# A planned instruction order for a recurrent attention and a mixing layer, searched again with other costs

## The chip, the cores and the metric

The kernel runs on one core of one Trainium2 chip. The metric is the device time of one execution in microseconds (us). The core's engines work side by side, each on its own queue of instructions in a fixed order: TensorE (PE, matmuls; PEld is its loading of weights), VectorE (DVE), ScalarE (ACT), GpSimd (POOL) and SyncE (SP, which here only issues DMAs). An instruction waits on semaphores for what other engines or DMAs have to finish first, and everything behind it in its queue waits too.

## The reference, cut to what matters

Two layers follow each other. The first is a recurrence over 768 tokens for 4 batches and 8 heads of width 48, the second mixes tokens and channels:

```python
for t in range(S):                       # r, k, v: [4, 8, 768, 48]
    cur = einsum('bhd,bhe->bhde', u[None] * kt, vt)
    y[:, :, t] = einsum('bhd,bhde->bhe', rt, state + cur)
    state = w[None, :, :, None] * state + einsum('bhd,bhe->bhde', kt, vt)
x = y.transpose(0, 2, 1, 3).reshape(4, 768, 384)
theta = x @ w_theta
zr, zi = x * cos(theta), x * sin(theta)
y = einsum('ts,bsd->btd', w_tok_r, zr) + einsum('ts,bsd->btd', w_tok_i, zi)
u = x + y
out = u + maximum(u @ w_ch, 0.0)         # float32
```

## The kernel before, in words

**Tiling.** The 768 tokens of a batch are three pairs of chunks of 128. The twelve pairs of the four batches are numbered g0 to g11; three make a batch. For each pair the recurrence is done in blocks. k and r are loaded (`ld`) and multiplied by tables of powers of the decay into `Kw` and `Rw` (line 677, "products"); eight 128x128 blocks of each are turned on TensorE (line 566, "flip") and copied out of PSUM as `KT` and `RT` (lines 575 and 577). `scores` (line 716) are KT times RT, masked by VectorE into `mAT` (line 723). `PD` (line 730) is the elementwise product of RT and KT; `diag` (line 739) sums it into a small bank that ScalarE copies as `dg`, and `yd` (line 747) is dg times v, the term with u. `outer` (lines 762 and 776) makes the pair's contribution to the state, and `Sb1`, `T`, `N` and `Sb0` carry the state on. `past` (line 836) and `outputs` (line 847) make the result, and `x` (line 855) adds yd. v is cast to bf16 as `vb` (lines 616 and 618); for g0 to g3, whose loads take two tokens to a partition, it is cast as `v2` (line 630), sorted by TensorE (`put`, line 641) and copied out (`put out`, lines 649 and 651).

The second layer takes x of a pair, turns it (on TensorE, or for g6 to g10 by a DMA that SP issues, "turn", line 586), multiplies by w_theta (`theta`, line 870), takes cosine and sine on ScalarE (lines 875 and 878) and multiplies x by both on VectorE (`z`, line 881). When z of a pair is there, a third of the token mixing of its batch can run: `mix` (line 901) is four matmuls of 384 columns, three such parts for each of six row blocks of 128 tokens. `un` (line 908) adds x, a DMA turns it (TensorE for g11), `chan` (line 924) multiplies by w_ch and `fin` (line 928) makes the output, which SP stores.

**Weights.** w_theta, w_tok_r, w_tok_i and w_ch are cast to bf16 by DMAs that GpSimd issues (line 523), behind a `gate` (line 701), a copy of one element that waits for the eighth load. Each cast of w_tok brings two row blocks (01, 23 or 45), which TensorE turns and ScalarE or VectorE copies out.

**What sets the order.** The kernel is first written down as 710 tasks with engine, cost, reads, writes and PSUM banks (`P.add`). `RANK` gives each task a priority and `MOVED` names the tasks that go to their other engine (`Plan.move`: copies out of PSUM, casts of v, products, PD and yd each have one). `Plan.order` then plays the program through with the planner's costs: an engine that is free takes, of the tasks that are ready, the one with the lowest priority value. The result is the order in which the instructions are written. The costs matter only for this. `act_ns`, `dve_ns` and `pool_ns` give them by the number of elements, a task on TensorE costs 1.9 times as much before `SLOW_UNTIL`, and of tasks marked `port=True` VectorE and GpSimd never run two at once in the plan. When the instructions are written, the first such GpSimd instruction after a VectorE one is made to wait for it (`add_manual_dep`, in the last loop); VectorE gets no such wait for GpSimd. `fill` (line 969) puts matmuls on a constant tile (`stuff`) where `replay` finds TensorE idle early on; their number in a gap goes by `FREE_FROM`.

Of the kernel before, what the change touches and what calls it, by code (L numbers as in the profile page):

```python
# [22 lines left out]
PE, DVE, ACT, POOL, SP = "PE", "DVE", "ACT", "POOL", "SP"  # L23
# [3 lines left out]
FILL_FIRST = 6  # L27
FILL_UNTIL = 17500.0
FREE_FROM = 7400.0
SLOW_UNTIL = 10400.0  # L30
TURN_LATE = 1300.0


# [6 lines left out]
class Plan:  # L40
# [50 lines left out]
    def order(self):  # L91
# [23 lines left out]
        while times or dma_next < math.inf:  # L115
# [26 lines left out]
            for e in engines:  # L142
# [14 lines left out]
                if e == PE:  # L157
                    ns += SWITCH if t.mode != last_mode else 0.0
                    ns *= 1.9 if now < SLOW_UNTIL else 1.0
                    last_mode = t.mode  # L160
# [33 lines left out]
CAST_AFTER = 7  # L194

RANK = [
# [38 lines left out]
]  # L235

MOVED = [
    32, 50, 74, 89, 97, 128, 165, 185, 198, 200, 213, 218, 225, 230, 246, 248, 249, 280, 285,
    358, 370, 371, 403, 405, 436, 448, 513, 526, 531, 573, 591, 606, 703,
]  # L240


# [8 lines left out]
def bc(ap, axis, n):  # L251
    new_ap = [list(x) for x in ap.ap]
    new_ap.insert(axis, [0, n])
    return dataclasses.replace(ap, ap=new_ap)
# [3 lines left out]
def kernel(  # L258
# [13 lines left out]
    nc = tc.nc  # L272
    B, H, S, D = r.shape
    HD = H * D
# [10 lines left out]
    P = Plan(8)  # L285
# [70 lines left out]
    def dve_ns(n, rate=1.0):  # L356
        return n / (0.96 * rate) + 66

    def pool_ns(n):
        return 190 + 1.95 * n  # L360

    def setup():
        P.add(SP, 420, lambda: nc.sync.dma_start(out=w_f, in_=w.rearrange("(o h) d -> o (h d)", o=1)),
# [232 lines left out]
    def front(b, base):  # L596
# [3 lines left out]
        for pr in range(NP):  # L600
# [24 lines left out]
            def cast2(eng, v2=v2, iv=slots[pr][2]):  # L625
# [5 lines left out]
                else:  # L631
                    eng.tensor_copy(dst, src)
            P.add(ACT, act_ns(2 * HD, False), lambda f=cast2: f(nc.scalar),
                  rd=both(slots[pr][2]), wr=[("v2", i2)], prio=base + 10 * pr + 1, name="v2",
                  alt=(POOL, pool_ns(2 * HD) - 200, True, lambda f=cast2: f(nc.gpsimd)))
            for c in range(2):
                tv = ("V", g, c)
# [18 lines left out]
        for pr in range(NP):  # L656
# [205 lines left out]
            xT, trig = xTs[g % 2], trigs[g % 2]  # L862
            turn(xT.rearrange("p t d c -> p (t d) c"), x[:, 2 * pr:2 * pr + 2],
                 ("TX", g), pb + 7, xk, [("xT", g % 2)], g in X_BY_DMA)
            for t in range(2):
                th = ("th", g, t)

                def theta(th=th, t=t, xT=xT):
# [9 lines left out]
                P.add(ACT, act_ns(HD) + 35, lambda th=th, t=t, trig=trig: nc.scalar.activation(  # L878
                    trig[:, t, 1], bank(th)[:, :HD], Act.Sin), use=[th],
                    wr=[("trig", g % 2, t, 1)], prio=pb + 8, name="sin")  # L880
            P.add(DVE, dve_ns(4 * HD, 2.0) + 80, lambda trig=trig, pr=pr: nc.vector.tensor_mul(  # L881
                z[:, 2 * pr:2 * pr + 2], bc(x[:, 2 * pr:2 * pr + 2], 2, 2), trig),
                rd=xk + [("trig", g % 2, t, i) for t in range(2) for i in range(2)],
                wr=[("z", zj, pr)] + (["w_f", "lw_f"] if g == NP else []), prio=pb + 9, port=True, name="z")
# [54 lines left out]

    setup()  # L940
    front(0, 0)
    for b in range(B):
        if b + 1 < B:
            front(b + 1, 100 * (b + 1))
        mixing(b, 100 * b + 150)
# [51 lines left out]
    for t in order:  # L997
# [8 lines left out]
        n = len(made)  # L1006
# [39 lines left out]
```

## Time and profile before

| | |
|---|---|
| median of 3 runs (lowest, highest) | 139.09 us (139.02, 139.81) |
| the profiled execution | 139.07 us, span 137.4 us, mean granted TensorE clock 0.996 |
| busy PE, DVE, ACT, POOL | 125.3, 112.3, 73.1, 62.5 us |
| moved by DMA | 25.24 MB, 184 GB/s on average |
| chain that ended last | PE 49%, DMA 17%, DVE 14%, POOL 9% |

The span runs from the first to the last instruction; the time of an execution holds 1.67 us more. "Busy" is the time in which an instruction of the engine was under way, which may include time in which it could not go on. The matmuls' ends are modelled: a matmul of 384 columns is shown with 0.326 us, and the next one starts 0.163 us after it. A row of the timeline gives start, length, engine, line, operation, tiles written and read, and in brackets how long the engine stood idle before it and what ended that. A row of a group gives count, busy time and the mean length in ns, then idle time before it.

### The profile page before, as it was taken

To read this page: it belongs to the slowest core of one execution; us is meant where nothing else is said; L and a number is where in the kernel's file an instruction comes from. 1 tells how busy PE (TensorE), PEld (TensorE's weight loads), DVE (VectorE), ACT (ScalarE), POOL (GpSimd) and SP (SyncE) were. 2 spreads that over 40 slices of the span, in tenths; PEclk is the share of its full clock that TensorE was granted. 3 is DMA by queue.
4 is the path that set the end of the run, shared out by engine and by line. 5 is a ranking of instruction groups with operands and counts; after the bars stand their busy time and mean duration, and the time that the engine had idled before them with its cause. 6 is when DMAs were issued, how large, how long until landed. Compare 5 with 4: busy or idle time off the path is not lost.

```text
span 137.4 us, 4145 instructions
## 1 busy us (share of the span) xinstructions
PE 125.3 (91%) x1698; PEld 84.9 (62%) x1698; DVE 112.3 (82%) x210; ACT 73.1 (53%) x137; POOL 62.5 (46%) x56
## 2 busy tenths in 40 slices
PE   1989888989999999999899997999899999999970
PEld 1567665776677667767566665776566666566640
DVE  6299999997888799998999999999855799454390
ACT  7996699999565660869334226457550092500010
POOL 7037999956080958776579909690000000000000
PEclk9999999999999999999999999999999999999998
DMA  2999999999979999999999999999991432526235
GB/s 69 235 325 325 315 194 198 196 196 202 219 153 237 154 224 105 207 199 185 180 149 224 165 229 225 199 250 175 197 289 36 88 107 95 139 93 172 57 149 195
DMA packets 72637, 25.24 MB, mean 184 GB/s; under 512 B 67241, under 2 KB 72618, under 8 KB 72618
## 3 DMA queue, kind: packets, MB, share of 16 engines
q1 hardware_dynamic: 70186, 22.03, 81.2%
q0 software_dynamic: 2432, 2.95, 12.5%
q8 instruction: 13, 0.21, 0.6%
q14 instruction: 6, 0.05, 0.1%
HBM read 20.06 MB, written 4.72 MB: 180 GB/s over the span
## 4 chain that ended last, share of the span: by engine, by line
PE 49%; DMA 17%; DVE 14%; POOL 9%; SPq 5%; issue 3%; ACT 1%; POOLq 0%; DVEq 0%
PE bank L901 24%; DMA z<-in_moe_w_tok_r_dram 7%; PE bank L566 6%; PE bank L870 6%; DMA ld<-in_v_dram 6%; PE bank L924 5%; SPq L503 4%; DVE mAT L723 4%; DMA ld<-in_r_dram 4%; POOL Rw L677 3%; DVE fin_all L928 2%; POOL yd L747 2%; PE bank L716 2%; PE bank L847 2%; PE bank L762 2%
## 5 line engine op out<-in xcount | busy, mean ns | idle before, releaser
L901 PE MATMUL bank<-z,WrT 128*128 128x384 bf16 x144 | 46.9, 326 | 0.0
L901 PE MATMUL bank<-z,WiT 128*128 128x384 bf16 x144 | 46.8, 326 | 0.0
L723 DVE TENSOR_TENSOR mAT<-bank,mask 128x512 bf16<-128x512 f32 x48 | 30.7, 680 | 1.4 <-PE bank L716 1.3
L677 POOL TENSOR_TENSOR Kw<-ld,kpow 128x768 bf16<-128x768 f32 x9 | 16.3, 1816 | 12.7 <-DVE PD L730 6.4
L908 DVE TENSOR_TENSOR uu_all<-bank,x 128x384 bf16<-128x384 f32 x24 | 13.3, 552 | 8.8 <-PE bank L901 8.3
L677 POOL TENSOR_TENSOR Rw<-ld,rpow 128x768 bf16<-128x768 f32 x9 | 16.4, 1820 | 7.1 <-DMA ld<-in_r_dram 3.4
L901 PEld LDWEIGHTS <-WrT 128*128 128x128 bf16 x144 | 14.0, 98 | 8.0
L901 PEld LDWEIGHTS <-WiT 128*128 128x128 bf16 x144 | 14.1, 98 | 7.8
L747 POOL TENSOR_TENSOR yd<-dg,vb 128x768 bf16<-128x768 f32 x10 | 14.7, 1477 | 6.8 <-DVE z L881 4.0
L878 ACT ACTIVATE trig<-bank 128x384 f16<-128x384 f32 x24 | 11.6, 494 | 10.2 <-PE bank L870 10.2
L928 DVE SCALAR_TENSOR_TENSOR fin_all<-bank,uu_all 128x384 f32<-128x384 f32 x24 | 12.6, 551 | 3.4 <-PE bank L924 3.4
L875 ACT ACTIVATE trig<-bank,pi 128x384 f16<-128x384 f32 x24 | 13.7, 584 | 1.9 <-PE bank L870 1.9
L870 PE MATMUL bank<-Wth,xT 128*128 128x384 bf16 x72 | 14.4, 326 | 0.4 <-DMA Wth<-in_moe_w_theta_dram 0.4
L924 PE MATMUL bank<-Wch,uu_all 128*128 128x384 bf16 x72 | 14.6, 326 | 0.0
L881 DVE TENSOR_TENSOR z<-x,trig 128x1536 bf16<-128x1536 bf16 x12 | 12.8, 1063 | 0.4 <-ACT trig L875 0.4
L855 DVE TENSOR_TENSOR x<-bank,yd 128x384 bf16<-128x384 f32 x24 | 12.3, 547 | 0.7 <-POOL yd L747 0.5
L577 ACT ACTIVATE KT<-bank 128x1024 bf16<-128x1024 bf16 (+1 forms) x10 | 9.8, 980 | 4.9 <-PE bank L566 3.9
L577 ACT ACTIVATE RT<-bank 128x1024 bf16<-128x1024 bf16 (+1 forms) x9 | 8.8, 976 | 4.2 <-PE bank L566 4.2
L924 PEld LDWEIGHTS <-uu_all 128*128 128x128 bf16 x72 | 6.7, 98 | 3.9
L566 PE MATMUL bank<-ident,Rw 128*128 128x128 bf16 x96 | 7.6, 220 | 1.6 <-DVE fin_all L928 0.8
L716 PE MATMUL bank<-RT,KT 64*128 64x128 bf16 x192 | 8.8, 218 | 0.0
L870 PEld LDWEIGHTS <-xT 128*128 128x128 bf16 x72 | 6.3, 97 | 4.0 <-issue 0.4
(108 smaller groups left out, 190.7 us busy)
## 6 DMA issues: line engine op xcount, KB each, us to landing
ld<-in_r_dram SPq DMA_DIRECT2D x12, 384.0 KB, 5.9
out_dram<-fin_all SPq DMA_DIRECT2D x11, 384.0 KB, 2.7
ld<-in_k_dram SPq DMA_DIRECT2D x16, 192.0 KB, 5.7
ld<-in_v_dram SPq DMA_DIRECT2D x16, 192.0 KB, 5.2
ld<-in_k_dram SPq DMA_DIRECT2D x4, 384.0 KB, 4.8
ld<-in_v_dram SPq DMA_DIRECT2D x4, 384.0 KB, 5.0
fin_all<-in_moe_w_tok_r_dram POOLq DMA_DIRECT2D x1, 384.0 KB, 8.6
x<-in_moe_w_tok_i_dram POOLq DMA_DIRECT2D x1, 384.0 KB, 10.1
```

The source lines that it names most:

```text
L566: nc.tensor.matmul(bank16(tok)[:, i * C:(i + 1) * C], s, ident, is_transpose=True, start=(i == 0), stop=(i == n - 1))
L577: nc.scalar.activation(dst, src, Act.Copy)
L677: eng.tensor_mul(X[:, :, hs, :D], src[:, :, hs], pw[:, :, hs])
L723: P.add(DVE, dve_ns(HP * C), lambda hi=hi, tk=tk, mAT=mAT: nc.vector.tensor_mul(mAT[:, hi], bank(tk[hi]).rearrange("p (h t) -> p h t", h=H ...
L747: eng.tensor_mul(yd.rearrange("p a h d -> p (a h) d"), wide(dg, D), vb.rearrange("p a h d -> p (a h) d"))
L870: nc.tensor.matmul(bank(th)[:, :HD], xT[:, t, dk, :], Wth[:, dk, :], start=(dk == 0), stop=(dk == ND - 1))
L875: P.add(ACT, act_ns(HD, False) + 65 + (1300 if g == 0 and t == 0 else 0), lambda th=th, t=t, trig=trig: nc.scalar.activation(trig[:, t, 0] ...
L881: P.add(DVE, dve_ns(4 * HD, 2.0) + 80, lambda trig=trig, pr=pr: nc.vector.tensor_mul(z[:, 2 * pr:2 * pr + 2], bc(x[:, 2 * pr:2 * pr + 2], ...
L901: nc.tensor.matmul(bank(tm)[:, :HD], (WrT, WiT)[ri][:, so, to * C:(to + 1) * C], z[:, so, ri], start=(part == 0 and i == 0), stop=(part == ...
L908: P.add(DVE, dve_ns(HD), lambda tm=tm, t=t, to=to, un=un: nc.vector.tensor_add(un[:, t], bank(tm)[:, :HD], x[:, to]), use=[tm], rd=[("x", ...
L924: nc.tensor.matmul(bank(tf)[:, :HD], uT[:, t, dk, :], Wch[:, dk, :], start=(dk == 0), stop=(dk == ND - 1))
L928: nc.vector.scalar_tensor_tensor(fin[:, t], bank(tf)[:, :HD], 0.0, un[:, t], op0=Alu.max, op1=Alu.add),
```

## The change

The planner's costs are changed in three places: TensorE is slow until 7400 ns instead of 10400, GpSimd's products cost 2.06 ns per element instead of 1.95, and VectorE's z costs 80 ns less. With these costs RANK and MOVED were searched anew, and both lists are replaced. Nothing that the tasks compute is changed.

```diff
-SLOW_UNTIL = 10400.0
+SLOW_UNTIL = 7400.0
@@ RANK: all 710 values replaced
-    0, 463, 462, 465, 464, 466, 467, 468, 471, 474, 479, 469, 472, 470, 473, 484, 607, 485, 486,
...
+    0, 331, 330, 333, 332, 334, 335, 336, 341, 344, 349, 337, 342, 338, 343, 354, 448, 358, 359,
...
 MOVED = [
-    32, 50, 74, 89, 97, 128, 165, 185, 198, 200, 213, 218, 225, 230, 246, 248, 249, 280, 285,
-    358, 370, 371, 403, 405, 436, 448, 513, 526, 531, 573, 591, 606, 703,
+    30, 74, 84, 97, 99, 112, 128, 131, 165, 177, 185, 212, 213, 218, 225, 230, 248, 251, 258,
+    261, 364, 371, 403, 439, 526, 538, 558, 561, 570, 591, 596, 606, 614, 701,
 ]
@@ def pool_ns(n):
-        return 190 + 1.95 * n
+        return 190 + 2.06 * n
@@ z
-            P.add(DVE, dve_ns(4 * HD, 2.0) + 80, lambda trig=trig, pr=pr: nc.vector.tensor_mul(
+            P.add(DVE, dve_ns(4 * HD, 2.0), lambda trig=trig, pr=pr: nc.vector.tensor_mul(
```

What this does to the engines: of the products Kw and Rw of whole pairs, VectorE does eight instead of four and GpSimd fourteen instead of eighteen; PD is eight on VectorE and four on GpSimd instead of ten and two; yd is three and nine instead of two and ten; all eight put out are on ScalarE instead of four; the cast v2 of g0 goes to GpSimd; of the vb casts VectorE does two instead of three; of the copies of turned blocks 13 instead of 12. The first instructions of each engine, up to the turning of g0's blocks, stay as they are but for two of ScalarE's table instructions, which go ahead of a copy. There are 22 filler matmuls instead of 21. In the DMA queue of SP the loads keep their order among themselves; turns and stores stand elsewhere between them.

74 rows, old and new, of the table RANK are left out of this document.

## The prediction

> **What bounds the kernel now.** First the busy table by stage of before (from and to in us, length, then busy time of PE matmul, PE weight load, DVE, ACT and POOL with their instruction counts, the granted TensorE clock, DMA share, GB/s):
>
> ```profile
> 0.00:10.00 10.00, 6.70 (x69) 4.71 (x69) 6.04 (x27) 8.74 (x19) 3.58 (x14) 1.00 0.77 206
> 10.00:30.00 20.00, 18.11 (x375) 13.68 (x373) 19.56 (x37) 17.10 (x33) 18.00 (x17) 1.00 1.15 241
> 30.00:50.00 20.00, 19.68 (x254) 13.76 (x255) 16.45 (x28) 14.48 (x27) 9.43 (x6) 1.00 1.04 193
> 50.00:70.00 20.00, 19.26 (x328) 13.56 (x327) 19.41 (x33) 10.77 (x22) 13.86 (x9) 1.00 1.27 178
> 70.00:100.00 30.00, 28.47 (x428) 19.00 (x427) 29.33 (x53) 13.41 (x25) 17.66 (x12) 1.00 1.22 206
> 100.00:130.00 30.00, 30.00 (x231) 18.45 (x230) 17.85 (x32) 8.07 (x17) 0.00 (x0) 1.00 0.44 119
> 130.00:138.00 8.00, 3.05 (x23) 1.76 (x21) 3.65 (x8) 0.49 (x1) 0.00 (x0) 0.90 0.39 147
> ```
>
> From 100 to 130 us TensorE has no gap: 30.00 of 30.00. What it still has to do there is fixed, so the end moves only if TensorE arrives at that stretch earlier or with less left. From 50 to 100 us VectorE paces it: 19.41 of 20 and 29.33 of 30, while TensorE is idle 0.74 and 1.53 us. From 30 to 50 us it is the other way round: TensorE 19.68 of 20, VectorE idle 3.55 us. From 10 to 30 us VectorE is full (19.56) and TensorE idles 1.89 us. So the kernel is worth what VectorE wastes before 100 us, and its idle 3.55 us at 30 to 50 is the one large reserve. Busy is not work, though. The timeline of DVE and of POOL shows a VectorE product that waits inside its own time:
>
> ```profile
> 65.23 0.95 DVE L881 TENSOR_TENSOR z<-x,trig 128x1536 bf16<-128x1536 bf16 x1
> ...
> 66.77 1.81 POOL L677 TENSOR_TENSOR Rw<-ld,rpow 128x768 bf16<-128x768 f32 x1 [2.65 <-DVE Sb L798]
> ...
> 67.10 2.30 DVE L881 TENSOR_TENSOR z<-x,trig 128x1536 bf16<-128x1536 bf16 x1
> ```
>
> The same product took 0.95 and 2.30: the long one began under GpSimd's and ended 0.8 us after it. Such a meeting costs up to 1.35.
>
> **The change, term by term.** The program has the same 710 tasks; engines and order differ. I go by landmarks: the work that stands ahead of one on its engine. Costs of VectorE's instructions, by form:
>
> ```profile
> L723 DVE TENSOR_TENSOR mAT<-bank,mask 128x512 bf16<-128x512 f32 x48 | 30.7, 680 | 1.4 <-PE bank L716 1.3
> L730 DVE TENSOR_TENSOR PD<-RT,KT 128x1024 bf16<-128x1024 bf16 x10 | 7.1, 707 | 0.1
> L575 DVE COPY RT<-bank 128x1024 bf16<-128x1024 bf16 x3 | 3.6, 1214 | 0.0
> L651 DVE CAST vb<-bank 128x384 bf16<-128x384 f32 x4 | 2.2, 550 | 0.3 <-PE bank L641 0.3
> L747 DVE TENSOR_TENSOR yd<-dg,vb 128x768 bf16<-128x768 f32 x2 | 1.9, 954 | 0.7 <-ACT dg L744 0.7
> L677 DVE TENSOR_TENSOR Rw<-ld,rpow 128x768 bf16<-128x768 f32 x2 | 1.9, 950 | 0.0
> L575 DVE COPY KT<-bank 128x1024 bf16<-128x1024 bf16 x2 | 1.4, 682 | 0.0
> L575 DVE COPY WiT<-bank 128x768 bf16<-128x768 bf16 x2 | 1.1, 558 | 0.9 <-PE bank L566 0.9
> ```
>
> And TensorE's tasks, from the chain of waits (start, length, what): six turned blocks, one mix (the first of all), two theta, one scores, one diag.
>
> ```profile
> 31.80 0.33 PE bank L566 x6
> 32.14 0.65 PE bank L901 x4
> ...
> 33.12 0.98 PE bank L870 x6
> ...
> 34.75 0.33 PE bank L716 x8
> ...
> 53.99 0.18 PE bank L739 x8
> ```
>
> *Term 1, TensorE up to batch 0's row block 4.* In before the last mix of block 4 stands behind two mixes of block 5, one diag and one scores of g5; in after it stands ahead of all four, and nothing else has moved across: 2 x 0.65 + 0.18 + 0.33 = 1.81 less. VectorE's work ahead of the sum that this mix feeds (un, line 908) is almost the same, by my count with these durations 45.6 before and 45.5 after. So VectorE is handed the same point 1.8 earlier; before used those 1.8 us up as idle time. **-1.8**, if TensorE is not late by then.
>
> *Term 2, TensorE at the first mix.* Here after may lose. The weights come through GpSimd's queue. The chain of waits of before shows four of its casts, and the DMA table their time to landing:
>
> ```profile
> 16.28 0.87 POOL Wth L523
> 17.16 0.74 POOL fin_all L523
> 17.90 0.71 POOL x L523
> ...
> 20.86 9.41 DMA z<-in_moe_w_tok_r_dram
> ```
>
> ```profile
> fin_all<-in_moe_w_tok_r_dram POOLq DMA_DIRECT2D x1, 384.0 KB, 8.6
> x<-in_moe_w_tok_i_dram POOLq DMA_DIRECT2D x1, 384.0 KB, 10.1
> ...
> Wth<-in_moe_w_theta_dram POOLq DMA_DIRECT2D x1, 288.0 KB, 6.4
> ```
>
> Landings: 17.16 + 8.6 = 25.8, 17.90 + 10.1 = 28.0, 20.86 + 9.41 = 30.3, one every 2.25 us however they are issued: a queue. The first mix needs the first pair of w_tok_r. In before that is the fourth cast, in after the fifth (the order is theta, tok_i 45, tok_r 23, tok_i 01, tok_r 01): +2.25. The queue also starts later, since on GpSimd the cast of g0's v comes first, Kw of g1 behind VectorE's new Rw of g1, and yd of g0 ahead of the gate instead of behind it:
>
> ```profile
> 9.11 0.69 DVE L575 COPY RT<-bank 128x512 bf16<-128x512 bf16 x1 [0.19 <-PE bank L566]
> 9.21 1.82 POOL L677 TENSOR_TENSOR Kw<-ld,kpow 128x768 bf16<-128x768 f32 x1 [5.44 <-DMA ld<-in_k_dram]
> ...
> 13.96 0.73 POOL L701 COPY gate<-ld 1x1 f32<-1x1 f32 x1
> 14.81 1.48 POOL L747 TENSOR_TENSOR yd<-dg,vb 128x768 bf16<-128x768 f32 x1
> ```
>
> By hand: VectorE's copy of RT ends at 9.8, PD 0.7 after it, uw at 10.7, Rw of g1 (0.95) at 11.7, GpSimd's Kw of g1 at 13.6, VectorE's Kw of g2 at 14.6, yd 16.1, gate 16.8, so theta's cast at 16.9 instead of 16.28: +0.6. The cast of v on GpSimd is not in the trace of before; between 0.73 (gate, one element) and 1.82 (Kw, two inputs of its size) I take 1.5, the nearest being yd; it moves theta's cast by 0.4 either way. Against these 2.85, TensorE has other work to do in the meantime: four turns of weights, two theta, a scores and a diag are now ahead of the first mix and two turns no longer: 2 x 0.33 + 0.98 + 0.33 + 0.18 = 2.15. So the first mix has 0.7 us more of idle time behind it. Between that mix (32.14) and block 4's last, before loses 0.32 by the table and, adding up the tasks' lengths, some 0.3 more that the modelled ends hide; after has VectorE further ahead there, and I take 0.6 as won back (bounds 0 and 0.6). **+0.1** (0.1 to 0.7; -0.5 if the casts start on time).
>
> The Trainium skill (SBUF — State Buffer, section "SBUF: two separate sides") has a rule against this term: a DMA issued from GpSimd's queue can't write its descriptors while VectorE holds the port that the two share, and after puts one product more (yd of g2, 0.95) on VectorE among the casts. By that rule the end would be up to 0.95 later, 138.4; the casts above took 0.71 to 0.87 with VectorE nearly full, so the trace doesn't show it.
>
> *Term 3, VectorE up to z of g7.* From block 4's sum on VectorE is the pace. Ahead of z of g7 it had 156 tasks and has 153: only before four evacuations of v (0.55), four PD, two Kw or Rw, one yd, three vb (0.55), two RT and one KT copies, one weight copy; only after one PD, six Kw or Rw, two yd, two vb, one RT copy, two weight copies, one small sum. The vb and the z of g7, from VectorE's timeline:
>
> ```profile
> 78.96 0.54 DVE L618 CAST vb<-ld 128x768 bf16<-128x768 f32 x1
> ...
> 97.62 0.95 DVE L881 TENSOR_TENSOR z<-x,trig 128x1536 bf16<-128x1536 bf16 x1
> ```
>
> With the rows: -2.2 -2.1 +3.8 +0.95 -0.55 -1.2 -0.7 +0.55 +0.35 = -1.1, and three instructions fewer cost less by 0.08 each, as VectorE starts the next early: **-0.8**. +0.35 is half a product's row for the small sum, whose tile is half an x. Meetings with GpSimd: I can't see those of after. GpSimd's total falls by four of 1.82 and a yd and rises by two PD and a v cast, but what falls goes to VectorE as products of the same kind; I take the same loss as before: **0** (from -1.4 to +2.7, one less or two more of 1.35).
>
> *Term 4, what TensorE has left.* At the mix that z of g7 releases, after has not yet done the turn of Rw of g11 (eight blocks at 0.055), its diag (0.18) and its outer (0.31 in the row below, 0.06 of it under the next): **+0.9**. That gives back what stands behind it in before:
>
> ```profile
> 98.29 0.84 ACT L616 ACTIVATE vb<-ld 128x768 bf16<-128x768 f32 x1 [1.29 <-DMA ld<-in_v_dram]
> ...
> 99.19 0.31 PE L762 MATMUL bank<-vb,Kw 128*64 128x48 bf16 x8 [0.43 <-ACT vb L616]
> ```
>
> In before TensorE waits 0.43 for the last v, whose load SP issued late behind the results of chan of g2; after does that chan twelve tasks sooner: **-0.4**.
>
> *Term 5, the last z.*
>
> ```profile
> 116.14 1.14 PE L870 MATMUL bank<-Wth,xT 128*128 128x384 bf16 x6
> ...
> 118.93 0.95 DVE L881 TENSOR_TENSOR z<-x,trig 128x1536 bf16<-128x1536 bf16 x1
> ```
>
> Six matmuls in 1.14 are one every 0.163, so TensorE goes on at 117.12, before the modelled end (117.28). From there to the end of z (119.88) are 2.76, and some 0.2 until TensorE can use it: 3.0. Before puts four mixes and a chan there (4 x 0.65 + 0.49 = 3.1), after four mixes only (2.6), but its two theta stand apart, which spares ScalarE about 0.1: **+0.3**. The tail behind it only swaps g9 with g10.
>
> *At nothing:* ScalarE gets four evacuations and loses a v cast and a small sum; it has 2.9 idle of 20 us there, and if that cover is gone each costs about 0.5. One filler matmul more in all, most of them still before 10 us: they run in gaps.
>
> Sum: -1.8 +0.1 -0.8 +0.9 -0.4 +0.3 = -1.7. The profiled execution took 139.07, span 137.4 and 1.67 around it; the median of the runs is 139.09. 139.07 - 1.7 = **137.4 us**.
>
> **Rivals.** *A. Nothing is won (139.0).* VectorE keeps the 1.8 and gives it back in one or two more meetings with GpSimd like that of 67.10 (1.35 each): 138.7 to 140.1. For: six Kw or Rw moved to VectorE are all of the shared kind, and the order of the two engines is only held one way (GpSimd waits for VectorE, not VectorE for GpSimd). Against: GpSimd has some 3 us less in all.
>
> *B. Slower: the weights are late.* GpSimd's first stretch is now one chain: Rw of g1, Kw of g1, Kw of g2, yd, gate, casts, each waiting for another engine, with four turns of weights in TensorE's queue ahead of work that is ready. If theta's cast goes out at 20.2 us instead of 16.9, the first mix and all behind it come 3.3 later: 137.4 + 3.3 = 140.7. It decides from 18.6 us on, where no gain is left. For: ScalarE is at 17.10 of 20 in that stretch and yd needs two of its outputs. Against: each wait has a row and the sum is 16.9.
>
> *C. The order does not get its clock.* It counts on full speed from 7.4 us instead of 10.4. If the clock fell between 10 and 33 us, TensorE's 18.11 us of tasks there would take up to twice their time; a fall that takes in 4 us of them costs up to 4 and gives up to 141.4. The table has 1.00 throughout in before. The Trainium skill (TensorE: Matmul & The Clock Gate, "Part 4: PE-mode transpose") says that transposes don't count as activity; by that rule the eleven turns that after has between the outputs of g1 and the first mix could let it fall. Before has nine there, six of them in 0.33 us, and 1.00 all the time, so I give it little.
>
> **How the numbers follow.** 1% is 1.4 us (137.7 and 140.5), about what a measurement of this kernel can tell from no change. Forecast (faster by over 1%) 0.48, where terms 1 and 3 hold; A 0.35; B 0.13; C 0.04. Range: below, one meeting less (-1.4) gives 136.0; above, two meetings more (+2.7) give 140.1 and the mild half of B 140.6: 136.0 to 140.6.
>
> **What would show it.** Right: VectorE idle under 2.5 us from 30 to 50 us; theta's cast between 16.5 and 17.5; z of g7 started near 95.1 instead of 97.62; no wait before the outer of g11; a gap of some 0.3 us on TensorE before the mixes of the last z. Wrong: a z or Kw of over 2 us on VectorE more than once (A), theta's cast after 18.6 or a gap of over 1 us before a turn of weights (B), a granted clock below 1.00 before 130 us (C), or a wait for a load between 50 and 90 us, which none of these has.

## The result, and the profile after

The changed kernel took 138.66 us (median of 18 executions, 137.59 to 140.62), the kernel before beside it 139.48 (138.61 to 140.42): a ratio of 0.993, 95% interval 0.990 to 0.996. So it is faster, by 0.8 to 0.9 us, about half of the 1.7 forecast. Ratios, here and below, leave out executions more than 1.5% above the fastest of the same kernel; medians and ranges are of all of them. The profiled execution: span 136.5 against 137.4, 138.24 us against 139.07.

Busy time by stage of the kernel after, in the columns of the prediction:

```profile
0.00:10.00 10.00, 6.89 (x36) 4.80 (x37) 5.64 (x26) 8.01 (x17) 3.61 (x14) 1.00 0.77 206
10.00:30.00 20.00, 19.51 (x401) 14.56 (x400) 19.24 (x36) 16.79 (x32) 14.95 (x16) 1.00 1.15 249
30.00:50.00 20.00, 19.70 (x287) 14.30 (x285) 18.54 (x31) 13.15 (x25) 9.75 (x6) 1.00 1.11 197
50.00:70.00 20.00, 19.71 (x300) 13.39 (x298) 19.49 (x35) 13.01 (x23) 10.42 (x7) 1.00 1.40 175
70.00:100.00 30.00, 28.54 (x428) 18.58 (x427) 26.22 (x46) 14.66 (x25) 19.74 (x13) 1.00 1.21 199
100.00:130.00 30.00, 30.00 (x246) 18.74 (x244) 20.83 (x36) 7.54 (x17) 0.00 (x0) 1.00 0.45 120
```

VectorE's idle time from 30 to 50 us fell from 3.55 to 1.46 us, as forecast. But from 70 to 100 us it rose from 0.67 to 3.78, and TensorE still loses 1.46 of 30 there. What was won by 50 us is partly lost by 100. Where, the timelines tell; VectorE first (start, length):

```profile
74.87 2.20 DVE L677 TENSOR_TENSOR Kw<-ld,kpow 128x768 bf16<-128x768 f32 x1
...
82.78 0.95 DVE L677 TENSOR_TENSOR Rw<-ld,rpow 128x768 bf16<-128x768 f32 x1
...
95.28 1.45 DVE L881 TENSOR_TENSOR z<-x,trig 128x1536 bf16<-128x1536 bf16 x1
99.31 0.36 DVE L798 TENSOR_TENSOR Sb<-bank,N 128x192 bf16<-128x192 f32 x1 [2.58 <-PE bank L762]
```

Kw of g8 met a product of GpSimd (2.20 instead of 0.95), and z of g7 met another (1.45). In brackets is the idle time ahead of an instruction and what ended it: most of VectorE's, 2.58 of the 3.78 us, lies behind z of g7, in a wait for TensorE's outer of g11. GpSimd's timeline of the same execution shows why they met:

```profile
72.67 1.82 POOL L677 TENSOR_TENSOR Kw<-ld,kpow 128x768 bf16<-128x768 f32 x1 [1.03 <-DMA ld<-in_k_dram]
74.45 1.82 POOL L677 TENSOR_TENSOR Rw<-ld,rpow 128x768 bf16<-128x768 f32 x1
...
94.10 1.82 POOL L677 TENSOR_TENSOR Kw<-ld,kpow 128x768 bf16<-128x768 f32 x1 [0.25 <-DMA ld<-in_k_dram]
```

GpSimd's Kw of g9 waited 1.03 us for its load, and began at 72.67, where before it began at 72.69 without such a wait, although VectorE was 2 us further on. On TensorE and ScalarE the same thing, a wait for a transfer:

```profile
90.56 0.66 PE L870 MATMUL bank<-Wth,xT 128*128 128x384 bf16 x3 [0.53 <-DMA xT<-x]
```

```profile
98.07 0.84 ACT L616 ACTIVATE vb<-ld 128x768 bf16<-128x768 f32 x1 [4.76 <-DMA ld<-in_v_dram]
```

ScalarE stood still for 4.76 us (1.29 before) and then cast g11's v at 98.07, where before it did so at 98.29; behind that cast TensorE's outer of g11 waited 0.52 us. These are the places that didn't move when everything ahead of them did.

### The profile page after: what moved, and what is told of

Read it like the earlier page. It is cut to its first block, busy times and chain, and to the rows that moved or that the text cites. A ratio compares the mean times of both kernels' runs of the same rounds, so it can differ in the third digit from the quotient of the medians.

```text
span 136.5 us, 4138 instructions
## 1 busy us (share of the span) xinstructions
PE 126.5 (93%) x1699; PEld 85.5 (63%) x1699; DVE 112.7 (83%) x210; ACT 73.6 (54%) x139; POOL 58.5 (43%) x54
## 2 busy tenths in 40 slices
DMA packets 72637, 25.24 MB, mean 185 GB/s; under 512 B 67241, under 2 KB 72618, under 8 KB 72618
## 4 chain that ended last, share of the span: by engine, by line
PE 58%; DVE 17%; DMA 10%; POOL 6%; issue 3%; ACT 2%; SPq 1%; DVEq 0%; POOLq 0%
PE bank L901 27%; PE bank L566 8%; PE bank L924 7%; PE bank L870 6%; DVE mAT L723 5%; DMA ld<-in_v_dram 4%; DMA xT<-x 4%; PE bank L716 3%; DVE Kw L677 3%; POOL Rw L677 3%; DMA ld<-in_r_dram 3%; PE bank L969 2%; PE bank L762 2%; PE bank L847 2%; DVE x L855 2%
## 5 line engine op out<-in xcount | busy, mean ns | idle before, releaser
L747 POOL TENSOR_TENSOR yd<-dg,vb 128x768 bf16<-128x768 f32 x9 | 13.3, 1473 | 12.0 <-DVE Rw L677 6.2
L677 POOL TENSOR_TENSOR Kw<-ld,kpow 128x768 bf16<-128x768 f32 x7 | 12.7, 1821 | 10.9 <-DVE PD L730 3.4
L677 POOL TENSOR_TENSOR Rw<-ld,rpow 128x768 bf16<-128x768 f32 x7 | 12.7, 1818 | 6.6 <-DVE Kw L677 4.0
L577 ACT ACTIVATE KT<-bank 128x1024 bf16<-128x1024 bf16 (+1 forms) x11 | 11.0, 996 | 5.9 <-issue 3.1
L730 POOL TENSOR_TENSOR PD<-RT,KT 128x1024 bf16<-128x1024 bf16 x4 | 8.5, 2123 | 5.2 <-DVE RT L575 3.3
L616 ACT ACTIVATE vb<-ld 128x768 bf16<-128x768 f32 x6 | 5.1, 844 | 7.2 <-DMA ld<-in_v_dram 7.2
```

Of the source, the lines that this page charges most:

```text
L577: nc.scalar.activation(dst, src, Act.Copy)
L677: eng.tensor_mul(X[:, :, hs, :D], src[:, :, hs], pw[:, :, hs])
L747: eng.tensor_mul(yd.rearrange("p a h d -> p (a h) d"), wide(dg, D), vb.rearrange("p a h d -> p (a h) d"))
```

## The experiments

The 18 runs come in five series, the last two on another chip. They are compared by their ratio to the kernel before, run beside each series, since its own median went from 138.9 to 139.8 between them. In the diffs, the list SHIFT gives tasks that are put behind another, or ahead of it, in the finished order; the loop that does it is shown once, and task numbers are explained beside them.

**First series: one meeting, two stores, both.** First the changed kernel itself.

> The changed kernel once more, as the measure for the others of this call. Both theories: 0.990 to 0.996 of before, span near 136.5. What it can also tell: whether the first flips (TR00, TK01, TR01) are slow again, about 0.60 us for four matmuls, or about 0.40 as in the profile of before. If they are fast this time, the cold beginning is chance from run to run and no part of the change.

0.996 (0.992 to 1.000), 138.68 us, and the first flips at 0.61 us again.

```diff
+SHIFT = [
+    (529, "after", 436),
+]
...
     order = P.order()
+    for seq, side, mark in SHIFT:
+        t = P.tasks[seq]
+        order.remove(t)
+        order.insert(order.index(P.tasks[mark]) + (side == "after"), t)
```

Task 529 is Rw of g9 (GpSimd), 436 is Kw of g8 (VectorE).

> Only Rw of g9 on GpSimd is held until VectorE's Kw of g8 is done. All theories: Kw of g8 takes 0.95 us instead of 2.20, and VectorE is 1.2 us ahead behind it. Theory (several limits in a row, at 75, 90, 97 and 99 us, each within 0.7 us of the next): TensorE still waits at theta of g7 for the turn of x on SyncE's queue and at outer of g11 for v, so the end moves by 0 to -0.3 us. Rival (VectorE is the pace up to 100 us, as the prediction's third term has it): the end moves by -0.9 us or more.

1.000 (0.996 to 1.003): nothing won, as the theory of several limits had it. Kw of g8 did take 0.95. But this profile also showed something that neither theory held. TensorE's clock fell. It fell in the profile of this series' last run too (both edits); here are the stages of that one, and its timeline of TensorE:

```profile
14.00:20.00 6.00, 5.76 (x145) 4.43 (x142) 6.00 (x13) 6.00 (x10) 5.53 (x6) 1.00 1.00 250
20.00:24.00 4.00, 1.97 (x48) 1.57 (x48) 3.61 (x7) 2.25 (x5) 3.98 (x4) 0.99 1.21 192
24.00:30.00 6.00, 5.89 (x75) 3.81 (x76) 3.83 (x8) 3.73 (x8) 4.90 (x6) 0.50 1.17 202
```

```profile
21.13 0.62 PE L572 MATMUL bank<-ident,Kw 128*128 128x128 bf16 x8 [1.14 <-POOL Kw L683]
...
24.11 1.14 PE L876 MATMUL bank<-Wth,xT 128*128 128x384 bf16 x3 [1.01 <-ACT dg L750]
```

The granted clock is 0.50 from 24 to 30 us, after TensorE had idled 2.03 of the 4 us before. This is rival C. In the list of executions it shows as a mean clock of 0.975 or less: 12 of the changed kernel's 30 executions have it (0.967 to 0.975). Of the 129 executions of the kernel before in the five series one is as low (0.967), and six lie at 0.980 to 0.984.

The stores:

```diff
+SHIFT = [
+    (338, "after", 521),
+    (352, "after", 524),
+]
```

Tasks 338 and 352 are the two stores; 521 and 524 the second load of g11's k and of its v.

> Only SyncE's order: the stores of the first two results of batch 1 stand behind the loads of g11's k and v instead of ahead of the turns. All theories: the turn of x of g7 and the loads of v of g11 are issued 0.5 to 1.1 us earlier, TensorE waits less at theta of g7 (0.7 before) and at outer of g11 (0.7 before). Theory (several limits in a row): z of g7, still late, takes over part; the end moves by -0.5 to -0.7 us. Rival (VectorE alone is the pace): z of g7 still begins at 95.3 and TensorE then waits for it, the end moves by less than 0.2 us.

0.991 (0.987 to 0.995), 137.53 us: -1.15 against the changed kernel of this series, more than the theory's -0.7, with only 1 fallen clock in 12. TensorE's wait for the turn of x is gone, that for v is 0.44 instead of 0.52.

> Both edits: Rw of g9 behind Kw of g8, and the stores behind the loads. Theory (several limits in a row): more than the two alone, -1.0 us or a little more against the changed kernel, TensorE's idle time at outer of g11 from 16.0 to 15.0 us. Rival (VectorE alone): no more than the first edit alone. Rival (SyncE's queue alone): no more than the second alone, -0.5 to -0.7.

0.994 (0.990 to 0.997), 6 of 12 with a fallen clock. Not more than the stores alone. No theory of mine gave that; the falls had to be taken out first.

**Second series: fewer fillers, and fillers at the gap.**

```diff
-fill(idle_from, t.start, int((until - since) / (214.0 if until < FREE_FROM else 110.0)))
+fill(idle_from, t.start, int((until - since) / 214.0))
```

> Filler matmuls of the beginning counted at 214 ns each, their duration while TensorE is cold: 14 instead of 22, 4 instead of 9 before the stand. Theory (what TensorE loses before 20 us is taken up by its waits for GpSimd's Kw of g3 and the weights at 21 to 24 us): in a cold beginning the stand comes up to 1.1 us earlier and the end stays, within 0.3 us of the changed kernel. Rival (the cold beginning is where the missing gain went): the end moves by -0.9 us.

0.998 (0.995 to 1.002), 5 of 12 fallen. Not a gain, so the cold beginning isn't where the missing gain went. The profiled execution was warm early (stand at 9.31 instead of 11.38), its clock fell, its first mix came at 36.61 instead of 34.42, but the first mix of the last z, at 120 us, only 0.2 later than in the profile of the changed kernel. That was the first sign that what VectorE gains before 75 us isn't worth its size at the end.

```diff
+EXTRA = {214: 8, 121: 2}
...
+for _ in range(EXTRA.get(t.seq, 0)):
+    nc.tensor.matmul(bank(t.acq[0])[:, :2 * C], stuff[:, :C], stuff, start=True, stop=True)
```

214 is the turn of g3's Kw, 121 the first theta.

> The changed kernel with eight filler matmuls ahead of the turn of Kw of g3 and two ahead of the first theta, where TensorE stood still for 1.1 and 0.5 to 1.0 us in the executions that had warmed up early. Theory (in some executions, 12 of 30 of the changed kernel by their mean clock of 0.967 to 0.975, the clock falls to 0.50 for 6.8 us from 23 or 24 us on, because of these gaps): at most 1 of 12 executions has a mean clock below 0.985, and the mean time falls by 0.2 to 0.4 us. Rival (the falls don't depend on these gaps, or cost nothing, as the VectorE-bound stage behind takes them up): falls as before in about 5 of 12, or the time unchanged or 0.3 worse for the fillers.

0.991 (0.987 to 0.995); no fallen clock in 12. In all runs with these fillers, the one with ScalarE's stores aside, 1 of 101 executions has a fall: the fillers take the falls away. What that is worth is less sure: the mean is 138.11 against 138.66 of the changed kernel's 30 executions (each to about 0.3 or 0.4), a difference hardly larger than its error. In its profile the gap is closed and the clock stays:

```profile
20.00:24.00 4.00, 4.00 (x95) 3.36 (x95) 3.83 (x8) 3.18 (x8) 3.58 (x4) 1.00 1.17 189
24.00:30.00 6.00, 6.00 (x120) 4.55 (x117) 5.90 (x11) 5.97 (x13) 5.19 (x6) 1.00 1.15 206
```

The next two put the first series' edits on top of these fillers.

> The same fillers, and the two stores of batch 1 behind the loads of g11's k. Theory: 136.9 to 137.3 us where before has 138.9, that is -1.3 to -1.6 against the changed kernel, the sum of the two edits. Rival (the gain of the stores alone came from having 1 fall in 12 executions by chance): no better than the fillers alone.

0.993 (0.990 to 0.997), 138.15 us: the stores add nothing to the fillers, as the rival had it. Its reason covers little, though: the two falls that the run with the stores had less than the changed kernel beside it (1 and 3 of 12) are worth 0.1 us, by the price of a fall found below. Why the stores won 1.15 us alone and nothing here stays open; the intervals of the two runs overlap.

> Fillers, stores, and Rw of g9 on GpSimd behind VectorE's Kw of g8. Theory (several limits in a row, the later ones, theta's turn and v of g11, being cleared by the stores): 0.4 to 0.8 us better than without the third edit. Rival (the meeting at 75 us is off the path, VectorE has reserve behind it): the same as without it, within 0.3.

0.991 (0.987 to 0.995), 137.85 us: 0.3 better than without the third edit, which the runs don't separate from nothing. It is faster than the kernel before; the 0.8 against the changed one (138.66) is not clear of noise, since the ratios, 0.991 and 0.993, have intervals that overlap. But where is the 1.25 us of the meeting? VectorE's and GpSimd's timelines:

```profile
75.81 0.95 DVE L684 TENSOR_TENSOR Kw<-ld,kpow 128x768 bf16<-128x768 f32 x1
...
82.96 2.07 DVE L684 TENSOR_TENSOR Rw<-ld,rpow 128x768 bf16<-128x768 f32 x1
```

```profile
80.98 1.81 POOL L684 TENSOR_TENSOR Kw<-ld,kpow 128x768 bf16<-128x768 f32 x1 [2.16 <-DMA ld<-in_k_dram]
```

Kw of g8 is short now, and Rw of g10, which took 0.95, takes 2.07. VectorE came to it at about the same time as in the changed kernel (82.96, there 82.78), GpSimd 1.4 us later: its Kw of g10 waited 2.16 us for a load, its yd of g8 behind it ran until 84.2, and VectorE's Rw of g10 met it. SyncE had issued that load no later (74.08, there 74.04), but it took 6.7 us to land instead of 5.1. The meeting moved by 7 us and cost 1.12 again.

**Third series: is VectorE the pace?** All but the last on the kernel just shown.

```diff
+    (344, "before", 341),
+    (345, "before", 341),
```

341 is block 4's last mix of batch 0, 344 and 345 the two of block 5.

> Against the kernel with fillers, stores and the held Rw (137.7 us, 0.991 of before): the two mixes of row block 5 of batch 0 stand ahead of block 4's last mix again, as in before. All theories: the sum of block 4 on VectorE begins 1.3 us later. The prediction's first term (what VectorE is handed later is the end later): +1.3 us, 139.0. Rival (from the first mix to 75 us one rigid block, behind which waits set by GpSimd's meetings and SyncE's queue take a delay up): +0.2 to +0.6.

0.991 (0.987 to 0.995), 137.95 us: +0.1, below even the rival's bound. The sum of block 4 began 1.33 later, the turn of Kw of g8 1.17 later, theta of g7 0.05 later. In between:

```profile
84.14 0.94 DVE L686 TENSOR_TENSOR Rw<-ld,rpow 128x768 bf16<-128x768 f32 x1
```

VectorE came 1.18 us later to Rw of g10, GpSimd was through with yd of g8, and the product was 1.13 shorter. Being early and being late end at the same time. TensorE shows it too: it idled 1.00 us from 50 to 60 us instead of 0.29, and nothing from 80 to 90, where it had lost 0.84.

```diff
...
-bc(mask01, 1, HP)),
+bc(mask01, 1, HP)) for _ in range(2 if g == 6 else 1)],
```

> The same kernel with the four masked products of g6's scores (mAT, 0.60 us each) done twice: VectorE has 2.4 us more between 60 and 66 us. VectorE as the pace up to 100 us: the end +2.4, 140.1 us. Rival (a delay there is taken up behind 75 us, as in the profiles with a fallen clock, where 2.2 us later at the first mix were 0.2 at 120 us): at most +1.0.

1.000 (0.998 to 1.003), 138.94 us: +1.1, half of the 2.4 put in, a little over the rival's bound. Rw of g10 is at 0.94 here too; 2.4 less 1.1 for the vanished meeting leaves 1.3.

```diff
-                P.add(SP, 500, lambda fin=fin, pr=pr, ts_=ts_: nc.sync.dma_start(
+                P.add(SP, 500, lambda fin=fin, pr=pr, ts_=ts_: (nc.scalar if b < 2 else nc.sync).dma_start(
```

> The same kernel with the stores of batches 0 and 1 issued by ScalarE, which is busy half of the time there, instead of SyncE. Theory (SyncE's queue, without a gap from 74 to 100 us, sets when x of g7 is turned and when g11's v is there): both issued 1 us or more earlier, the wait for v ahead of outer of g11 gone, end -0.3 to -0.7 us. Rival (SyncE is no longer a limit once the two stores stand back): within 0.3 us of 137.7, or later, as ScalarE waits for results of chan.

1.019 (1.015 to 1.024), slower. ScalarE's timeline shows its first store, and what stood behind it:

```profile
67.35 0.42 ACTq L941 DMA_DIRECT2D out_dram<-fin_all  x1
67.81 0.49 ACT L885 ACTIVATE trig<-bank 128x384 f16<-128x384 f32 x1 [4.56 <-DMA ld<-in_v_dram]
```

ScalarE idled 4.56 us until that store could go, a wait that the profile puts down to a transfer, and TensorE then waited 3.46 us for its copy of RT; its clock fell there too. So the run says that ScalarE has no room for a store that waits, and nothing of SyncE's queue.

```diff
+SHIFT = [
+    (439, "after", 310),
+]
```

This one is on the kernel before: 439 is Rw of g8, 310 z of g5.

> The kernel before, with Rw of g8 on GpSimd held until VectorE's z of g5 is done. All theories: z of g5 takes 0.95 us instead of 2.30, GpSimd's Kw of g8 ends 0.4 later. The prediction's price of a meeting (1.35 at the end, less 0.4 for Kw of g8): -0.9 us. Rival (taking one meeting away shifts the engines against each other and makes another, as Rw of g10 grew from 0.95 to 2.0 where Kw of g8 had shrunk): within 0.4 us of before.

1.010 (1.007 to 1.013): slower by 1.4. z of g5 took 0.95, and TensorE paid for it, as its timeline shows:

```profile
71.14 0.62 PE L570 MATMUL bank<-ident,Rw 128*128 128x128 bf16 x8 [2.20 <-POOL Rw L681]
```

The held Rw of g8 began at 69.28 instead of 66.77 and its turn on TensorE waited 2.20 us (0.35 before). A meeting of 1.35 was cheaper than the wait that avoids it.

**Fourth series: the load taken off SyncE's queue.** On the kernel with all three edits:

```diff
-issue(lambda c=c: nc.sync.dma_start(
+issue(lambda c=c: (nc.gpsimd if src is k and (b, pr) == (3, 1) else nc.sync).dma_start(
...
+    (514, "after", 386),
+    (515, "after", 514),
```

514 and 515 are the loads of g10's k, 386 is GpSimd's yd of g6.

> The kernel with fillers, stores and held Rw, and the two loads of g10's k issued by GpSimd at 63.6 us instead of by SyncE at 73 to 75. Theory (this load is the limit of the stage): Kw of g10 no longer waits 2.16 us for it, yd of g8 ends before VectorE's Rw of g10, which takes 0.95 instead of 2.07, and what SyncE issues after 75 us comes up to 2 us earlier: 136.5 to 137.0 us (0.983 to 0.986 of before). Rival (another limit follows at once): within 0.3 us of 137.7.

0.999 (0.996 to 1.003): 0.8% worse than without the edit. GpSimd's timeline:

```profile
74.86 1.81 POOL L686 TENSOR_TENSOR Kw<-ld,kpow 128x768 bf16<-128x768 f32 x1 [2.41 <-DMA ld<-in_k_dram]
```

g10's k was there in time, but now g9's k, issued by SyncE 0.5 us later than in the changed kernel (65.27 against 64.80), was there 2.2 later (74.86 against 72.67). What one load gained the other lost, so it isn't SyncE's turn that was short.

> The same without holding Rw of g9. Theory: Kw of g10 waits for nothing but VectorE, Kw of g8 meets Rw of g9 if VectorE is not ahead of it (0.2 to 1.4 us): 136.7 to 137.5 us. Rival (holding is what counts): 0.5 or more above the run with the held Rw.

0.999 (0.995 to 1.003), the same with or without the held Rw.

> The changed kernel with this edit alone, no fillers, stores as they were. Theory (SyncE's queue set theta of g7's turn and v of g11): -0.6 to -1.0 us against the changed kernel, as with the stores; some executions still with a fallen clock. Rival: within 0.3 us of the changed kernel (138.66).

0.998 (0.991 to 1.004), but from three executions only; the median of all 12 is 140.62, 1.0 above the kernel before, and 4 of them have a fallen clock. No gain, and too scattered for more.

> As the first of these, with the two mixes of row block 5 ahead of block 4's last again, so that VectorE is handed the sum 1.3 us later. Theory (with the load out of the way VectorE paces up to 97 us): 0.8 to 1.3 us above the first of these. Rival (slack elsewhere took it up): within 0.3 us of it.

0.992 (0.988 to 0.996): no later than the first of these, rather earlier. The price of term 1 did not come back, so my candidate, this one load, fell.

**Fifth series: fewer bytes.** The last candidate stands on the page of the profile, in its line of the DMA engines' busy share (tenths, 40 slices of 3.4 us), here after:

```profile
DMA  2999999999999999999999999999994623506245
```

From 3.4 to 102 us all slices are at nine tenths or more. In before it was so too, but for one slice at 7.

```diff
+nh = H // 2 if src is v and 7 <= NP * b + pr <= 10 else H
...
-out=Ls[i][:, c, :, :D],
-in_=rows.rearrange("h (c p) d -> c p h d", c=2)[c]), [("L", i, c)], 1220)
+out=Ls[i][:, c, :nh, :D],
+in_=rows.rearrange("h (c p) d -> c p h d", c=2)[c][:, :nh]), [("L", i, c)], 1220)
```

> The kernel with fillers, stores and held Rw; of the v of g7 to g10 only half of the heads is loaded (the other half keeps what the buffer held), which takes 1.5 MB in eight transfers to 0.75 MB. Theory (the DMA engines, full up to 95 us, limit the stage from 72 us on): GpSimd's Kw of g10 waits for no load, the turn of x of g7 and v of g11 come 1.5 to 3 us earlier, the end -0.8 to -2 us against 137.7, or 0.977 to 0.985 of before. Rival (VectorE or the order of GpSimd and VectorE limits whatever the loads do): within 0.4 us, 0.988 to 0.994.

0.978 (0.974 to 0.982), 136.71 us, in the theory's range and well outside the rival's. Half of v was left out of four groups, so this time isn't a kernel's that could be used; it tells what these loads cost, 1.3% against the same kernel with all of v, by the ratios of two series. GpSimd, ScalarE and the stages:

```profile
79.40 1.82 POOL L685 TENSOR_TENSOR Kw<-ld,kpow 128x768 bf16<-128x768 f32 x1 [0.98 <-DVE PD L738]
```

```profile
94.59 0.85 ACT L624 ACTIVATE vb<-ld 128x768 bf16<-128x768 f32 x1 [2.23 <-DMA ld<-in_v_dram]
```

```profile
75.00:100.00 25.00, 25.00 (x375) 16.82 (x373) 21.53 (x40) 13.85 (x25) 16.26 (x10) 1.00 1.11 211
```

Kw of g10 waits for VectorE and no load, Rw of g10 takes 0.95, g11's v is cast at 94.59 instead of 97.88, and TensorE has no gap from 75 to 100 us, where it lost 0.84 with all of v. That gap is the surer measure: of the 1.5 us between the two profiles 0.5 was there at the first mix (34.81 instead of 35.33), ahead of the first load that was halved (55.88). The share of the DMA engines, on the other hand, hardly tells the two apart: 1.11 from 75 to 100 us, and 1.18 with all of v.

> The same with half of v, and the two mixes of row block 5 ahead of block 4's last. Theory (with fewer bytes VectorE is the pace again, so the price of term 1 comes back): 0.8 to 1.3 us above the run before it. Rival (no limit of the loads, or the meetings take it up): within 0.4 us of it.

0.987 (0.981 to 0.992), 137.76 us: +1.05. Here the 1.3 us of term 1 do cost most of their size, as the theory said. The two intervals just touch, but the profiles agree: TensorE idled 1.00 us from 50 to 60 us instead of 0.30, had no gap from 60 to 100 in either, and the span is 0.7 longer. The first mix happened to be 0.5 us earlier in this one, so block 4's sum began only 0.9 later; of this 0.7 is there at the turn of Kw of g8, at z of g7 (95.42 instead of 94.72) and at the first mix of the last z. With all of v, 0.05 of 1.33 had been left at theta of g7.

## Why the prediction was wrong

The direction was right and the range held the time, but the gain was about half of the forecast. The step that failed is the first sentence drawn from the table: that "the kernel is worth what VectorE wastes before 100 us", with VectorE as the pace from block 4's sum on. What VectorE gained by 50 us it gave back behind it, in waits for TensorE and in meetings with GpSimd, and from 72 us on transfers set when GpSimd, ScalarE and TensorE could go on.

- **Term 1, -1.8.** The hand-over did come early: TensorE began block 4's last mix at 51.94 instead of 54.04, and the idle reserve of 30 to 50 us was used. Its price at the end was wrong: undoing 1.3 of it cost 0.1 us with the loads as they are (each ratio is good to 0.4%, some 0.6 us), 1.05 with less to load.
- **Term 2, +0.1.** About right, in part by errors that cancel. Theta's cast went out at 17.30 (16.9 forecast; 16.7 to 17.7 in the other profiles of the new order): yd of g0 began 1.2 us later than summed up, behind a wait of 1.51 for ScalarE, and the gate took 0.18 instead of 0.73. TensorE's longest waits between 20 and 36 us in the profile after are 0.34 and 0.30, both for GpSimd's products and none for a weight. The first mix came 2.45 later, 0.3 more than the 2.15 of work put ahead of it (+0.7 forecast there, of which 0.6 was to be won back). The rule of the Trainium skill (SBUF — State Buffer, section "SBUF: two separate sides") gave 138.4, near the measured 138.66, but not by its mechanism: after theta's 0.94 the casts took 0.72 to 0.76 us with VectorE full, as before.
- **Term 3, -0.8, meetings 0.** z of g7 began at 95.28, 95.1 forecast, by two errors that cancel: block 4's sum began 2.34 us earlier (52.88, before 55.22), not 1.7, and from there to z VectorE took 42.40 us in both kernels, not 0.8 less. Its work did shrink (the rows add up to -0.86, put down as -0.8): it was busy 41.91 us in before and 41.01 in after. Its idle time grew by as much, from 0.49 to 1.39, and 1.13 of that are waits for TensorE, the longest 0.47 at 57.52 and 0.32 at 73.94. So VectorE was not the pace of the whole stretch. The price of 0 for the meetings holds there: Kw of g8 lost 1.25 and two PD and a cast of v 0.8, in before z of g5 1.35 and two casts of v 1.3. Then z of g7 itself met one, +0.5. But meetings aren't chance with a fixed price, as I took them: they follow from which engine waits for what, they move when taken away (Kw of g8 to Rw of g10), and holding GpSimd out of one made the kernel before slower by 1.4.
- **Term 4.** The +0.9 was there. The -0.4 was not: the load of g11's v was issued 1.4 us earlier and cast 0.2 earlier; it took 6.3 us to land, 4.9 in before. Moving the chan of g2 ahead moved SyncE's queue, not the arrival.
- **Term 5, +0.3.** No gap: TensorE's matmuls run on every 0.16 us through z of g11 at 118.58.
- **Rival C, 0.04.** It came in 12 of 30 executions. I had read the profile of before as proof that the clock holds; it is one execution; where the changed order is warm early, TensorE runs ahead and then waits at 20 to 24 us. The price was over-stated as much as the chance was under-stated: up to 4 us by the prediction, 0.6 (with a standard error of 0.3) between the changed kernel's executions with a fall (mean 139.0) and without (138.4). The stage behind takes most of it up: in the three profiles with a fall in the first two series the first mix comes at 36.45 to 37.03, but TensorE idles only 0.6 us from 30 to 100, where it idles 2.05 in the profile after.
- **Rivals A and B.** A named meetings that give the gain back. They are there, and they move, but VectorE loses no more in them than in before, and A's sign, a z or Kw of over 2 us more than once, did not come: only Kw of g8 is that long. B didn't occur.
- **What would make it wrong.** "A wait for a load between 50 and 90 us" was named, and is there at 72.67. The table that I quoted could have warned me: its DMA share is highest in these stages, 1.27 and 1.22, and I read only its engines. It could not have given the price, since the share is above 1 in every stage from 10 to 100 us.

By the profiled execution, 0.8 of the 1.7 is missing. TensorE's own account says where. From 100 to 130 us it has no gap in either kernel, so what counts is its idle time ahead of that. From 30 to 100 us it idled 2.59 us in before and 2.05 in after, where the forecast needed some 2 us less (the 1.7, and 0.3 for a gap at the last z that did not open). Of the 2.05, 0.53 is the wait for the turn of x and 0.52 that for v, both transfers, and 0.41 lies between 70 and 80 us, 0.3 of it a wait for Kw of g8. z of g7's own meeting shows no price: TensorE has no gap from 91.2 to 98.4 us, as far as its modelled ends tell. How much each wait would be worth without the others stays open, since the edits of the first two series didn't add up. That less to load takes the waits away, and gives VectorE's lead its worth back, is shown for the kernel with all three edits; for the changed kernel itself it is argued from the same waits. Half of v is also 4096 packets less of 72637, and less on SyncE's queue. The run that moved a load off that queue speaks against the queue; bytes and packets are not told apart.

## What to carry to other kernels

Price a lead by the idle time that it can take from the engine that is full up to the end, here TensorE, and not by the idle time of the engine that gains it. And ask what comes by transfers in the same stage: work that comes earlier may only wait for its load or meet another engine, and an edit that takes one collision away can find it again a few microseconds on. A high share of the DMA engines is a warning and not a proof; test it with fewer bytes, which is one small edit, before moving more instructions. And read the clock from all executions, not from one profile: a new order can open gaps that trip it in some of them, and a few filler matmuls in the gap are cheap.

## What the runs showed of the hardware

The clock fell to 0.50 after gaps of no more than 1.14 us, two of them within 4 us, for 6.8 us each time (23.24 to 30.07 in one profile, 23.92 to 30.75 in another), and in 12 of 30 executions of the changed kernel. The Trainium skill (TensorE: Matmul & The Clock Gate, section "HAM oscillation — how this bites in real kernels") puts the rule as no idle gap over some 3.4 us; here shorter gaps were enough, and the measurement decides. That page's window of about 3.4 us fits the length of the fall, twice 3.4.

The gaps alone don't decide. With the stores alone, TensorE has gaps of 1.14 and 0.54 us at the same places, and the clock stays. The traces record when the clock was granted, and in all five profiles with a fall before 130 us it begins a whole number of steps of 3.41 us after the first grant: five steps in four of them (6.17 to 23.24 us in the first above), 18 in the run with ScalarE's stores (7.60 to 69.04), where TensorE had stood still for 3.46 us and the fall lasts one step. In the step ahead of the four, TensorE was busy for 0.58 to 0.67 of the time. With the stores alone the gap of 1.14 us lies across the border of two steps, busy for 0.77 and 0.71. But in other runs steps of 0.53 to 0.66, between 62 and 80 us, passed without a fall, so what else decides stays open.

The granted clock is 1.00 in the rows of the first 12 us, but the matmuls aren't always at full speed there: the record of the clock begins only at 11.46 us in the profile after and at 6.69 in that of the kernel with fillers and stores, and the rows show 1.00 where there is none. Nine fillers of one shape took 2.13 us in one execution and 1.15 in another:

```profile
9.32 2.13 PE L969 MATMUL bank<-stuff 128*128 128x256 bf16 x9
```

```profile
8.54 1.15 PE L979 MATMUL bank<-stuff 128*128 128x256 bf16 x9
```

The first is of the kernel after, the second of the one with fillers and stores. The first mix came at 34.42 and 34.32: a beginning that is 1.8 us slower costs nothing by then.
